# Hedgehog attention and Mish layers on one core: reordering the norm, the key folds and a statistic in the first block

## The chip, the core and the metric

The program runs on one core of a Trainium2 chip. The trace names its engines PE (TensorE, matmul), PEld (its weight loads), DVE (VectorE), ACT (ScalarE), POOL (GpSimd) and SP (SyncE, which issues all transfers here). Each engine works through its own queue in the order in which the compiled program holds it, and stops at an instruction whose wait is not yet fulfilled; nothing behind that instruction on the same engine goes ahead of it. The metric is the device time of one launch in microseconds (us), the median of several.

## The reference

The input `x` has 2048 rows of 640 numbers. Twice over, two layers are applied to it, each of them added to its own input:

```python
x = x + A(layernorm(x))      # linear attention with the Hedgehog feature map
x = x + B(layernorm(x))      # dense 640 -> 1536, Mish, dense 1536 -> 640
```

In A, `q`, `k` and `v` are 32 heads of 20 columns each, from one product with `wqkv`. For queries and keys, each head's 20 numbers are multiplied by the head's own 20x20 matrix `w_phi`, and the features are the softmax of the result beside the softmax of its negative. Then `kv = phi_k^T v` and `z = sum(phi_k)` over all rows, the output is `phi_q kv / (phi_q z)`, and `wo` follows.

## The kernel before

All rows are worked in 8 blocks of 256 rows (`NB`), a block being two tiles (`BT`) of 128 rows. Each fp32 operand of a product is split in a high part and the rest (`hi`, `lo`, tiles ending in h and l), and a product is three matmuls in a narrower form: high by high, high by low, low by high. So 128 rows by 640 columns of depth into one half of the columns takes 5 x 3 = 15 matmuls (`project_half`, L385); a `project` (L376) does both halves. Their rows in the trace are L391.

`w_phi` does not act on the features. It is folded into the query and key weights once, at the start: for each of the 5 row blocks `k` of the weights, and for each half `c` of their columns, `fold_part` (L257) issues three matmuls of a block of `wqk_t` with the block diagonal of `w_phi` (L262 in the trace; each is recorded as two). I call this fold (k,c). `fold_end` (L272) then evicts the fold's bank: ACT copies it to the high weights (L275), and DVE subtracts that copy from the bank to get the low weights (L276). The query weights are `r2h`, `r2l`, the key weights `r1h`, `r1l`; the right 640 columns of the `r1` tiles are the value weights.

PSUM is used in two kinds of tiles: two `mm` tiles of two banks each, and four `one` tiles of one bank. The framework that records the program puts in the waits: an instruction that writes an `mm` tile waits for what was recorded earlier and reads or writes that tile, the other bank included.

The order of work at the start of layer 0 (`attend_first`, L435):

- Written out by hand (`with written()`, L500 to 557): load x of block 0, the statistics of its rows on DVE (`norm_stats`) with their scaling on POOL (`norm_scale`), fold the first halves of the query weights, normalise the two tiles of rows (`xn`: one on ACT at L529, one on DVE at L530), turn them on PE (`Transposed.step`, L325, with the copies L330/L331), the first half of the first query product `q0`, fold the second halves of the query weights beside the splitting of the value weights (`make_v`, L142/L143), and the second half of `q0`.
- From L565 on, the loop over blocks. Its order within a queue is made by a planner that simulates the block of code with costs of its own (`schedule_with_timeline_sim`); `issue_after` gives it an order that it has to keep. Block 0 takes `q0, v0, v1, k0, q1, k1`. `fold_phi(kv_ws, ...)` folds the key weights between `v1` and `k0`: 10 folds, (0,0) (1,0) (2,0) (3,0) (0,1) (1,1) (2,1) (3,1) (4,0) (4,1), even `k` in the two banks of an `mm` tile and odd `k` in two `one` tiles.
- Beside these, for each coming block its x is loaded, its statistics are taken (`fetch_normed`, L438: four `BATCH_NORM_STATS2` of L295 on DVE, two aggregates of L297, three small steps on POOL, two scalings of L307 on DVE), its rows are normalised on ACT (L134) and turned on PE.
- `features` (L402) makes phi of one tile of rows: an ACT copy out of PSUM, two reductions (L416), two subtractions (L417, L419), an exponential on ACT, a sum (L425), a reciprocal (L426) and a product on POOL (L427).

The second layer and all later stages (attend_second, dense) have the same order before and after the change.

Of the kernel before, what the change touches and what calls it, by code (L numbers as in the profile page):

```python
# [1 line left out]

# [6 lines left out]
F32 = mybir.dt.float32  # L9
F32R = mybir.dt.float32r  # L10
AF = mybir.ActivationFunctionType
ALU = mybir.AluOpType
# [32 lines left out]
def kernel(  # L45
# [22 lines left out]
    def mm_tile():  # L68
        return psum.tile([P, 2, 512], F32, tag="mm", name="mm", bufs=2)

    def one_tile():
        return psum.tile([P, 512], F32, tag="one", name="one", bufs=4)
# [41 lines left out]
    x1_d = dram.tile([S, D], F32, name="x1_d")  # L114
    x2_d = dram.tile([S, D], F32, name="x2_d")

    last_act, in_written, last_low, last_load, last_recip = [None], [False], [None], [None], [None]

    @contextmanager
    def written():  # L120
# [136 lines left out]
    def fold_part(ps, k, t, bd, raw):  # L257

        r, rows = raw[t]
        heads = rows // DH  # L260
        n = DL * (6 * (t % 3) if t < 5 else 10)
        nc.tensor.matmul(ps[:, n:n + heads * DL].rearrange("p (j d) -> p j d", d=DL), r[:rows, k * P:(k + 1) * P],  # L262
                         bd[:rows, t, :rows].rearrange("p (j d) -> p j d", d=DH)[:, :, :DL], start=True, stop=True)

    def shift_phi(bd, ts):

# [5 lines left out]
    def fold_end(ws, ps, k, c):  # L272
        n0, n1 = (0, 18 * DL) if c == 0 else (18 * DL, QK)
        hi, lo = ws[k][0][:, n0:n1], ws[k][1][:, n0:n1]
        nc.scalar.activation(hi, ps[:, :n1 - n0], AF.Copy)  # L275
        nc.vector.tensor_tensor(lo, ps[:, :n1 - n0], hi.bitcast(F32), op=ALU.subtract)  # L276

    def fold_phi(ws, bd, raw):

        pss = {}  # L280
        for k, c in ((0, 0), (1, 0), (2, 0), (3, 0), (0, 1), (1, 1), (2, 1), (3, 1), (4, 0), (4, 1)):
            if c == 0:
                mm = None if k % 2 else mm_tile()
                pss[k] = [one_tile(), one_tile()] if k % 2 else [mm[:, 0], mm[:, 1]]
            ps = pss[k][c]
            for t in range(3 * c, 3 * c + 3):
                fold_part(ps, k, t, bd, raw)
            fold_end(ws, ps, k, c)


# [9 lines left out]
    def norm_scale(b, mvs):  # L300

        ve = work.tile([P, BT], F32, tag="ve", name="ve", bufs=2)
        for t in range(BT):
            nc.gpsimd.tensor_scalar(ve[:, t:t + 1], mvs[t][:, 1:2], LN_EPS, 1.0, op0=ALU.add, op1=ALU.mult)
        nc.gpsimd.tensor_tensor(stats[:, b, 0], ve, neg_half, op=ALU.pow)
        for t in range(BT):
            nc.vector.scalar_tensor_tensor(stats[:, b, 1, t:t + 1], mvs[t][:, 0:1], -1.0,  # L307
                                           stats[:, b, 0, t:t + 1], op0=ALU.mult, op1=ALU.mult)
# [76 lines left out]
    def project_half(ps, xts, t, ws, col, c, ks=range(KD), w=HC):  # L385
        sl = slice(t * P, (t + 1) * P)
        cs = slice(col + c * w, col + (c + 1) * w)
        for k in ks:
            h, l, wh, wl = xts.hs[k], xts.ls[k], ws[k][0][:, cs], ws[k][1][:, cs]
            for n, (a, r) in enumerate(((h, wh), (h, wl), (l, wh))):  # L390
                nc.tensor.matmul(ps[:, :w], a[:, sl], r, start=(k == 0 and n == 0),  # L391
                                 stop=(k == KD - 1 and n == 2))

    def both(ps, w=HC):

# [39 lines left out]
    def attend_first(layer, x_src, first):  # L435


        def fetch_normed(b):  # L438
            if layer:
                return load_turned(n2_d[b], [row_tile] * 3, nc.gpsimd)  # L440
            xt = fetch(x_src, b) if b > 1 else early
            norm_scale(b, [norm_stats(t, xt) for t in range(BT)])
            return xt

        pending = []
# [53 lines left out]
        if first is None:  # L499
            with written():  # L500
                xt = fetch(x_src, 0)
                bd = big_tile()[:120, :720].rearrange("p (t c) -> p t c", t=6)
                nc.sync.dma_start(bd[:, :3], phi_bd[:, :3])
                raw_q = load_raw(0, range(3))

                nc.vector.memset(bd[:80, 5, :80], 0.0)
                nc.sync.dma_start(bd[:40, 5, :40], phi_bd[80:120, 4, 80:120])
                nc.sync.dma_start(bd[40:80, 5, 40:80], phi_bd[:40, 5, :40])
                nc.sync.dma_start(bd[:, 3:5], phi_bd[:, 3:5])
                shift_phi(bd, slice(0, 3))  # L510
                raw_q += load_raw(0, range(3, 6))
                kv_ws = [r1_pair(k) for k in range(KD)]
                raw_v = [fetch_v(k) for k in range(KD)]
                raw = load_raw(1)
                early = fetch(x_src, 1)
                mvs = [norm_stats(t, xt) for t in range(BT)]
                norm_scale(0, mvs)
                shift_phi(bd, slice(3, 5))
                shift_phi(bd, 5)

                q_ws = [r2_pair(k) for k in range(KD)]
                mm = [mm_tile(), mm_tile()]
                pcs = [mm[0][:, 0], mm[0][:, 1], mm[1][:, 0], mm[1][:, 1], one_tile()]
                for t in range(3):
                    for k in range(KD - 1):
                        fold_part(pcs[k], k, t, bd, raw_q)
                fold_end(q_ws, pcs[0], 0, 0)
                xn = [row_tile() for _ in range(BT)]
                act(xn[0], xt[:, 0, :], AF.Identity, bias=stats[:, 0, 1, 0:1], scale=stats[:, 0, 0, 0:1])  # L529
                nc.vector.tensor_scalar(xn[1], xt[:, 1, :], stats[:, 0, 0, 1:2], stats[:, 0, 1, 1:2],  # L530
                                        op0=ALU.mult, op1=ALU.add)
                fold_end(q_ws, pcs[1], 1, 0)
                fold_end(q_ws, pcs[2], 2, 0)
                nxt = Transposed(xn)
                nxt.step()
                fold_end(q_ws, pcs[3], 3, 0)
                nxt.step()
                for t in range(3):
                    fold_part(pcs[4], 4, t, bd, raw_q)
                nxt.step()  # L540
                fold_end(q_ws, pcs[4], 4, 0)
                mm = mm_tile()
                q0 = [mm[:, 0], mm[:, 1], mm]
                project_half(q0[0], nxt, 0, q_ws, 0, 0, w=QC)

                def make_v(k):
                    split(kv_ws[k][0][:, D:2 * D], kv_ws[k][1][:, D:2 * D], raw_v[k])

                for k in range(KD):
                    ps = one_tile()  # L550
                    for t in range(3, 6):
                        fold_part(ps, k, t, bd, raw_q)
                    fold_end(q_ws, ps, k, 1)
                    if k > 0:
                        make_v(k - 1)
                project_half(q0[1], nxt, 0, q_ws, 0, 1, w=QC)
                make_v(KD - 1)
            nc.sync.dma_start(mask, bass.AP(tensor=head_mask.tensor, offset=head_mask.offset,
                                            ap=[[1, 120], [120 * (DH + 1), 3]]))
        else:  # L560
            nxt, kv_ws, turn = first
            with tc.issue_after(last_load[0]):
                load_k_weights(kv_ws)
            q_ws = load_q_weights()
        for b in range(NB):  # L565
# [15 lines left out]
            for n, (kind, t) in enumerate(order):  # L581
                t = int(t)
                i = b * BT + t
                if b == 0 and n == (1 if layer else 3):
                    if layer == 0:
                        fold_phi(kv_ws, bd, raw)
                    kva = one_tile()
                    nc.vector.memset(kva[:, :360], 0.0)
                if b == NB - 1 and n == 3:
                    loaded = {0: load(0)}  # L590
                if b + 1 < NB:
                    if n == 0:
                        xt = fetch_normed(b + 1)
                    elif n == 2:
                        nxt = xt if layer else normed(b + 1, xt)
                    elif n > 2:
                        nxt.step()
                g = {"k": lambda: keys(xts, i, vs[t]), "q": lambda: queries(xts, i, q0 if i == 0 and not layer else None),
                     "v": lambda: values(xts, i, vs[t])}[kind]()
                if b == NB - 1 and n == 3:  # L600
                    advance()
                    next(g)
                else:
                    next(g)
                    if layer and b == 0 and n == 0:
                        turn()
                    advance()
                pending.append(g)
# [414 lines left out]
```

## Time and profile before

| what | value |
|---|---|
| median of 3 runs | 1363.8 us (1362.54 to 1365.35) |
| the profiled execution | 1361.69 us, its span 1359.7 us |
| PE busy | 1349.6 us, 99% of the span |
| DVE busy | 1057.4 us, 78% |
| ACT busy | 576.0 us, 42% |
| POOL busy | 464.0 us, 34% |
| transfers | 174.11 MB, mean 128 GB/s |

The profile has several views: the page with the busy time of each engine and the span cut in slices, the list of waits (who stood still, and what ended it), and the timeline (the instructions of an engine in order of time: start, duration, engine, line, operation, output <- input, shape, count of merged instructions, and in brackets the idle time ahead of it with what ended it). A duration in the timeline overlaps the next instruction's start a little, so the distance between two starts is the better price of a step in a full queue. Most of the change lies in the first 50 us of 1360.

### The profile page before, as it was taken

To read this page: it belongs to the slowest core of one execution; us is meant where nothing else is said; L and a number is where in the kernel's file an instruction comes from. 1 tells how busy PE (TensorE), PEld (TensorE's weight loads), DVE (VectorE), ACT (ScalarE), POOL (GpSimd) and SP (SyncE) were. 2 spreads that over 40 slices of the span, in tenths; PEclk is the share of its full clock that TensorE was granted. 3 is DMA by queue.
4 is the path that set the end of the run, shared out by engine and by line. 5 is a ranking of instruction groups with operands and counts; after the bars stand their busy time and mean duration, and the time that the engine had idled before them with its cause. 6 is when DMAs were issued, how large, how long until landed. Compare 5 with 4: busy or idle time off the path is not lost.

```text
span 1359.7 us, 30969 instructions
## 1 busy us (share of the span) xinstructions
PE 1349.6 (99%) x12896; PEld 1338.2 (98%) x12896; DVE 1057.4 (78%) x1799; ACT 576.0 (42%) x967; POOL 464.0 (34%) x417
## 2 busy tenths in 40 slices
PE   9999999999999999999999999999999999999998
PEld 9999999999999999999999999999999999999998
DVE  5888988876687887778769788779668776676775
ACT  4444344322454545445443334332236444444443
POOL 2355644444222222222225555634351211111111
PEclk9999999999999999999999999999999999999999
DMA  9543443797714442244563534559964221233200
GB/s 338 156 103 79 98 96 81 206 287 274 222 40 98 117 117 69 61 106 100 145 209 81 119 79 91 96 120 289 289 246 125 78 72 39 86 98 97 73 26 20
DMA packets 352629, 174.11 MB, mean 128 GB/s; under 512 B 287449, under 2 KB 324041, under 8 KB 352489
## 3 DMA queue, kind: packets, MB, share of 16 engines
q1 hardware_dynamic: 352489, 172.14, 46.7%
q8 instruction: 101, 1.65, 0.5%
q14 instruction: 39, 0.32, 0.1%
HBM read 106.23 MB, written 65.86 MB: 127 GB/s over the span
## 4 chain that ended last, share of the span: by engine, by line
PE 94%; DVE 3%; POOL 1%; ACT 0%; issue 0%; DVEq 0%; POOLq 0%
PE mm L391 25%; PE mm L851 25%; PE one L809 25%; PE one L391 12%; PE mm L686 3%; PE one L325 2%; PE one L464 2%; DVE r L425 1%; DVE m L416 0%; DVE r L419 0%; POOL big L427 0%; DVE big L417 0%; DVE r1l L276 0%; POOL xtl L331 0%; POOL r L427 0%
## 5 line engine op out<-in xcount | busy, mean ns | idle before, releaser
L851 PE MATMUL mm<-r2h,ol 128*128 128x320 f32 x1280 | 304.8, 309 | 0.0
L835 POOL TENSOR_TENSOR ol<-big,ol 128x512 fp32r<-128x512 f32 (+1 forms) x98 | 131.1, 1338 | 477.2 <-ACT ol L834 419.1
L809 PE MATMUL one<-xtl,r1h 128*128 128x256 f32 x960 | 268.2, 279 | 0.0
L809 PE MATMUL one<-xth,r1l 128*128 128x256 f32 x960 | 268.0, 279 | 0.0
L809 PE MATMUL one<-xth,r1h 128*128 128x256 f32 x960 | 265.9, 279 | 0.0
L851 PEld LDWEIGHTS mm<-r2h,ol 128*128 128x128 f32 x1280 | 219.2, 188 | 0.0
L851 PE MATMUL mm<-r2l,ol 128*128 128x320 f32 x640 | 197.3, 309 | 0.0
L391 PE MATMUL mm<-r1h,xth 128*128 128x304 f32 (+1 forms) x600 | 185.1, 309 | 1.5 <-DVE r1l L276 1.5
L391 PE MATMUL mm<-r1l,xth 128*128 128x304 f32 (+1 forms) x600 | 183.8, 306 | 0.0
L391 PE MATMUL mm<-r1h,xtl 128*128 128x304 f32 (+1 forms) x600 | 183.5, 306 | 0.2 <-POOL xtl L331 0.2
L809 PEld LDWEIGHTS one<-xtl,r1h 128*128 128x128 f32 x960 | 180.4, 188 | 0.0
L809 PEld LDWEIGHTS one<-xth,r1l 128*128 128x128 f32 x960 | 180.4, 188 | 0.0
L809 PEld LDWEIGHTS one<-xth,r1h 128*128 128x128 f32 x960 | 179.6, 188 | 0.0
L824 DVE TENSOR_SCALAR big<-big 128x512 f32<-128x512 f32 (+1 forms) x98 | 56.6, 578 | 110.0 <-ACT big L822 109.8
L851 PEld LDWEIGHTS mm<-r2l,ol 128*128 128x128 f32 x640 | 120.2, 188 | 0.0
L834 ACT ACTIVATE ol<-big 128x512 fp32r<-128x512 f32 (+1 forms) x98 | 60.9, 622 | 137.8 <-DVE big L833 137.8
L826 ACT ACTIVATE big<-big,two 128x512 f32<-128x512 f32 (+1 forms) x98 | 70.1, 716 | 116.0 <-DVE big L825 115.9
L822 ACT ACTIVATE big<-one,b1s 128x256 f32<-128x256 f32 x192 | 80.9, 468 | 88.5 <-PE one L809 88.0
L427 POOL TENSOR_TENSOR r<-r,r 128x1280 f32<-128x1280 f32 x32 | 77.2, 2413 | 119.1 <-DVE r L426 101.6
L391 PEld LDWEIGHTS mm<-r1h,xth 128*128 128x128 f32 x600 | 112.8, 188 | 2.6 <-DVE r1l L276 1.7
L391 PEld LDWEIGHTS mm<-r1h,xtl 128*128 128x128 f32 x600 | 112.8, 188 | 0.4 <-POOL xtl L331 0.4
L391 PEld LDWEIGHTS mm<-r1l,xth 128*128 128x128 f32 x600 | 112.8, 188 | 0.1
(142 smaller groups left out, 3118.0 us busy)
## 6 DMA issues: line engine op xcount, KB each, us to landing
e_d<-r SPq DMA_DIRECT2D x128, 160.0 KB, 4.0
big<-e_d SPq DMA_DIRECT2D x32, 640.0 KB, 7.6
x_d<-xt SPq DMA_DIRECT2D x23, 640.0 KB, 3.8
xt<-x_d SPq DMA_DIRECT2D x22, 640.0 KB, 5.5
n_d<-xn SPq DMA_DIRECT2D x168, 80.0 KB, 2.3
xt<-in_x SPq DMA_DIRECT2D x16, 640.0 KB, 4.4
xn<-x_d SPq DMA_DIRECT2D x28, 320.0 KB, 4.4
v<-n_d SPq DMA_DIRECT2D x30, 256.0 KB, 3.1
```

The lines of the kernel that those rows point to most:

```text
L325: nc.tensor.transpose(ps[:, c, t * P:(t + 1) * P], self.rows[t][:, (c0 + c) * P:(c0 + c + 1) * P], ident)
L391: nc.tensor.matmul(ps[:, :w], a[:, sl], r, start=(k == 0 and n == 0), stop=(k == KD - 1 and n == 2))
L427: nc.gpsimd.tensor_tensor(eg, eg, r.unsqueeze(2).to_broadcast([P, 2 * H, DH]), op=ALU.mult)
L464: nc.tensor.matmul(kva[32 * j:32 * j + DH + 1, 40 * r:40 * r + 40], v[:, (DH + 1) * h:(DH + 1) * (h + 1)], e[:, 40 * h:40 * h + 40], start ...
L686: nc.tensor.matmul(po[64 * q:64 * q + 64, c, GW * j:GW * j + w], phs[g][:n, s0:s0 + 64], kvb[:n, g, :w], start=True, stop=True)
L809: nc.tensor.matmul(ph[:, j, :], l, r, start=(n == 0), stop=(n == 3 * KD - 1))
L822: exps[0] = nc.scalar.activation(part(ta, 0)[:, j - js.start], ph[:, j, :], AF.Exp, bias=b1s[:, 2 * pr + j:2 * pr + j + 1]).ins
L824: nc.vector.tensor_scalar_min(e, e, E_CAP)
L826: nc.scalar.activation(r, n, AF.Ln, bias=two)
L834: nc.scalar.activation(ah[:, js], n, AF.Copy)
L835: nc.gpsimd.tensor_tensor(al[:, js], n, ah[:, js].bitcast(F32), op=ALU.subtract)
L851: nc.tensor.matmul(pys[t][:, c, :HC], l[:, j, sl], r, start=(f == 0 and n == 0), stop=(f == KF - 1 and n == 2))
```

## The change

It has four parts, all in layer 0, block 0:

1. The two normalisations `xn` of block 0 stand ahead of the eviction of query fold (0,0) instead of behind it.
2. The key folds go in two groups. The folds (0,0) (1,0) (2,0) (3,0) go ahead of `v1`, the other six, (4,0) (0,1) (1,1) (2,1) (3,1) (4,1), behind it. In each group the first four go into the four banks of the two `mm` tiles, in that order; the last two of the second group go into `one` tiles.
3. `issue_after` now holds each fold and each product of block 0 behind the product recorded before it (`last_product`), and, for the last two steps of the block, the pending feature work behind the last key eviction (`last_fold`).
4. The statistics of block 3 are held behind the last key eviction.

```diff
-    def fold_phi(ws, bd, raw):
-        pss = {}
-        for k, c in ((0, 0), (1, 0), (2, 0), (3, 0), (0, 1), (1, 1), (2, 1), (3, 1), (4, 0), (4, 1)):
-            if c == 0:
-                mm = None if k % 2 else mm_tile()
-                pss[k] = [one_tile(), one_tile()] if k % 2 else [mm[:, 0], mm[:, 1]]
-            ps = pss[k][c]
-            for t in range(3 * c, 3 * c + 3):
-                fold_part(ps, k, t, bd, raw)
+    def fold_phi(ws, bd, raw, parts):
+        mm = [mm_tile(), mm_tile()]
+        banks = [mm[0][:, 0], mm[0][:, 1], mm[1][:, 0], mm[1][:, 1]]
+        for n, (k, c) in enumerate(parts):
+            ps = banks[n] if n < 4 else one_tile()
+            with tc.issue_after(last_product[0]):
+                for t in range(3 * c, 3 * c + 3):
+                    fold_part(ps, k, t, bd, raw)
             fold_end(ws, ps, k, c)
...
-            norm_scale(b, [norm_stats(t, xt) for t in range(BT)])
+            with (tc.issue_after(last_fold[0]) if b == 3 else nullcontext()):
+                norm_scale(b, [norm_stats(t, xt) for t in range(BT)])
...
-                fold_end(q_ws, pcs[0], 0, 0)
                 xn = [row_tile() for _ in range(BT)]
                 act(xn[0], xt[:, 0, :], AF.Identity, bias=stats[:, 0, 1, 0:1], scale=stats[:, 0, 0, 0:1])
                 nc.vector.tensor_scalar(xn[1], xt[:, 1, :], stats[:, 0, 0, 1:2], stats[:, 0, 1, 1:2],
                                         op0=ALU.mult, op1=ALU.add)
+                fold_end(q_ws, pcs[0], 0, 0)
...
+                if b == 0 and layer == 0 and n in (2, 3):
+                    fold_phi(kv_ws, bd, raw, ((0, 0), (1, 0), (2, 0), (3, 0)) if n == 2 else
+                             ((4, 0), (0, 1), (1, 1), (2, 1), (3, 1), (4, 1)))
                 if b == 0 and n == (1 if layer else 3):
-                    if layer == 0:
-                        fold_phi(kv_ws, bd, raw)
                     kva = one_tile()
...
-                if b == NB - 1 and n == 3:
+                if b == 0 and not layer:
+                    with tc.issue_after(last_product[0]):
+                        next(g)
+                    with (tc.issue_after(last_fold[0]) if n > 3 else nullcontext()):
+                        advance()
+                elif b == NB - 1 and n == 3:
```

The compiled programs hold the same instructions on each engine. Their orders differ in the first 50 us alone. This is how the queues of the changed program stand in the part that matters (line numbers of the kernel before; "evict" is a fold's ACT copy or DVE subtraction):

```
PE   query folds (0,1)..(4,1) | q0 second half, 15 | v0, 30 | fold (0,0) | fold (1,0) | fold (2,0) | fold (3,0)
     | v1, 30 | folds (4,0) (0,1) (1,1) (2,1) (3,1) (4,1) | 4 transposes | k0, 30 | 4 transposes | q1, 30 | 2 transposes | k1
DVE  ...splitting of the value weights | 4 stats of block 1 | 2 reductions L416 of q0 | 2 aggregates
     | 4 stats of block 2 | L419 of q0 | aggregate | evict (0,0) | 2 scalings L307 | aggregate | 2 scalings L307
     | evict (1,0) (2,0) (3,0) | L425 of q0 | evict (4,0) | L426 of q0 | evict (0,1) (1,1) | memset
     | evict (2,1) (3,1) (4,1) | transpose of q0 | 4 stats of block 3 | L331 | ...
ACT  copy of q0 | ones column | 2 copies of v0 | evict (0,0) | 2 normalisations of block 1 | ones column
     | evict (1,0) (2,0) (3,0) | 2 copies of v1 | exponential of q0 | evict (4,0) (0,1) (1,1) (2,1) (3,1) (4,1) | ...
```

And these waits stand in the changed program on PE: fold (1,0) waits for the DVE eviction of fold (0,0), fold (3,0) for that of (2,0), fold (0,1) for that of (4,0), fold (2,1) for that of (1,1). In the kernel before, fold (2,1) waits for the DVE eviction of (2,0) in the same way. On SP the writes of the folded key weights (`wp_d`, L222) go in another order, and all ten stand ahead of the four writes of q0's features (`e_d`, L481); before, the two writes of the last row block and one load of `wo` (L156) stood behind those four.

More of the change, by code (lines that the diff above doesn't have):

```diff
@@ L1 @@
-from contextlib import ExitStack, contextmanager
+from contextlib import ExitStack, contextmanager, nullcontext
 import concourse.bass as bass
@@ L115 @@
     x2_d = dram.tile([S, D], F32, name="x2_d")
-    last_act, in_written, last_low, last_load, last_recip = [None], [False], [None], [None], [None]
+    last_act, in_written, last_low, last_load, last_recip, last_fold, last_product = (
+        [None], [False], [None], [None], [None], [None], [None])
     @contextmanager
@@ L261, in fold_part @@
         n = DL * (6 * (t % 3) if t < 5 else 10)
-        nc.tensor.matmul(ps[:, n:n + heads * DL].rearrange("p (j d) -> p j d", d=DL), r[:rows, k * P:(k + 1) * P],
+        ins = nc.tensor.matmul(ps[:, n:n + heads * DL].rearrange("p (j d) -> p j d", d=DL), r[:rows, k * P:(k + 1) * P],
                          bd[:rows, t, :rows].rearrange("p (j d) -> p j d", d=DH)[:, :, :DL], start=True, stop=True)
+        last_product[0] = ins.ins
     def shift_phi(bd, ts):
@@ L275, in fold_end @@
         nc.scalar.activation(hi, ps[:, :n1 - n0], AF.Copy)
-        nc.vector.tensor_tensor(lo, ps[:, :n1 - n0], hi.bitcast(F32), op=ALU.subtract)
-    def fold_phi(ws, bd, raw):
-        pss = {}
-        for k, c in ((0, 0), (1, 0), (2, 0), (3, 0), (0, 1), (1, 1), (2, 1), (3, 1), (4, 0), (4, 1)):
-            if c == 0:
-                mm = None if k % 2 else mm_tile()
-                pss[k] = [one_tile(), one_tile()] if k % 2 else [mm[:, 0], mm[:, 1]]
-            ps = pss[k][c]
-            for t in range(3 * c, 3 * c + 3):
-                fold_part(ps, k, t, bd, raw)
+        last_fold[0] = nc.vector.tensor_tensor(lo, ps[:, :n1 - n0], hi.bitcast(F32), op=ALU.subtract).ins
+    def fold_phi(ws, bd, raw, parts):
[6 more added lines that the diff above has]
+                    fold_part(ps, k, t, bd, raw)
             fold_end(ws, ps, k, c)
@@ L390, in project_half @@
             for n, (a, r) in enumerate(((h, wh), (h, wl), (l, wh))):
-                nc.tensor.matmul(ps[:, :w], a[:, sl], r, start=(k == 0 and n == 0),
-                                 stop=(k == KD - 1 and n == 2))
+                last_product[0] = nc.tensor.matmul(ps[:, :w], a[:, sl], r, start=(k == 0 and n == 0),
+                                                   stop=(k == KD - 1 and n == 2)).ins
     def both(ps, w=HC):
```

## The prediction

> **What bounds the kernel now.** I read the page first, then PE's list of waits, then the timeline of each engine over the first 60 us.
>
> ```profile
> span 1359.7 us, 30969 instructions
> PE 1349.6 (99%) x12896; PEld 1338.2 (98%) x12896; DVE 1057.4 (78%) x1799; ACT 576.0 (42%) x967; POOL 464.0 (34%) x417
> PEclk9999999999999999999999999999999999999999
> ...
> PE mm L391 <- DVE r1l L276: 1.5, 1, 1.5
> PE mm L262 <- DVE r1l L276: 1.1, 1, 1.1
> PE one L325 <- ACT xn L131: 0.9, 1, 0.9
> PE mm L686 <- issue: 0.4, 1, 0.4
> ```
>
> PE is the bound, at full clock in all slices. Once it has started it stands still for 1.5 + 1.1 + 0.9 us in block 0, all in what the change touches, and for under 1 us in the other 1300 us. This says two things. The change can gain at most some 3.5 us (0.26%). And whatever idle time it gives PE comes out at the end in full, because no later slack takes it up. So the question is what PE waits for in the new order.
>
> ```profile
> 15.24 0.56 PE L262 MATMUL one<-big,raw 120*128 120x114 f32 x4
> ...
> 24.43 0.31 PE L391 MATMUL one<-r1l,xth 128*128 128x320 f32 x1
> 30.00 0.31 PE L391 MATMUL one<-r1h,xtl 128*128 128x320 f32 x1
> 30.15 0.82 PE L262 MATMUL one<-big,raw 120*128 120x114 f32 x6
> 30.80 0.83 PE L262 MATMUL mm<-big,raw 120*128 120x114 f32 x6
> ...
> 35.34 0.67 PE L262 MATMUL mm<-big,raw 120*128 120x114 f32 x4 [1.05 <-DVE r1l L276]
> 39.47 0.41 PE L391 MATMUL mm<-r1h,xth 128*128 128x304 f32 x1 [1.49 <-DVE r1l L276]
> 44.44 0.30 PE L391 MATMUL mm<-r2h,xth 128*128 128x304 f32 x1
> ```
>
> Prices from here: a value matmul 0.147 us (38 steps between 24.43 and 30.00), so a `v` of 30 is 4.4; a fold 0.65 (30.15 to 30.80); `k0` 4.2 (39.47 to 44.44 is 4.97 for its 30 matmuls with fold (4,1) of 0.65 among them, and 0.1 goes to the restart). The row of 35.34 is fold (2,1) waiting for the DVE eviction of (2,0), which lies in the other bank of its `mm` tile. That wait, 1.05 us, is the one that the new order meets four times. The row of 39.47 is `k0` waiting for an eviction that stood behind block 3's statistics:
>
> ```profile
> 20.68 0.43 DVE L276 TENSOR_TENSOR r2l<-one,r2h 128x266 fp32r<-128x266 f32 x1
> 24.16 1.67 DVE L295 BATCH_NORM_STATS2 bn<-xt 128x6 f32<-128x320 f32 x4 [1.15 <-DMA xt<-in_x]
> 25.75 0.33 DVE L297 BATCH_NORM_AGGREGATE mv<-bn 128x2 f32<-128x12 f32 x2
> 25.99 0.87 DVE L295 BATCH_NORM_STATS2 bn<-xt 128x6 f32<-128x320 f32 x2
> 26.78 1.53 DVE L416 TENSOR_REDUCE m<-r 128x32 f32<-128x640 f32 x2
> 28.23 0.88 DVE L295 BATCH_NORM_STATS2 bn<-xt 128x6 f32<-128x320 f32 x2
> 29.22 0.82 DVE L419 TENSOR_TENSOR r<-m,r 128x640 f32<-128x640 f32 x1
> 29.95 0.20 DVE L297 BATCH_NORM_AGGREGATE mv<-bn 128x2 f32<-128x12 f32 x1
> 31.24 0.23 DVE L307 SCALAR_TENSOR_TENSOR stats<-mv,stats 128x1 f32<-128x1 f32 x2 [1.09 <-POOL stats L305]
> 32.96 1.49 DVE L425 TENSOR_REDUCE r<-r 128x64 f32<-128x1280 f32 x1 [1.48 <-ACT r L134]
> 34.36 0.50 DVE L276 TENSOR_TENSOR r1l<-one,r1h 128x342 fp32r<-128x342 f32 x1
> 37.48 1.61 DVE L295 BATCH_NORM_STATS2 bn<-xt 128x6 f32<-128x320 f32 x4
> 39.00 0.42 DVE L276 TENSOR_TENSOR r1l<-mm,r1h 128x266 fp32r<-128x266 f32 x1
> ```
>
> DVE is full from 24.16 on, when x of block 1 lands, and works in queue order. Starts give the prices: four statistics 1.59, two aggregates 0.24, two reductions 1.45, L419 0.73.
>
> **The change part by part.** All times are on the clock of the profiled execution before.
>
> *Norm ahead of the eviction.*
>
> ```profile
> 9.55 0.46 ACT L275 ACTIVATE r2h<-mm 128x342 fp32r<-128x342 f32 x1 [7.55 <-PE mm L262]
> 10.04 0.51 DVE L276 TENSOR_TENSOR r2l<-mm,r2h 128x342 fp32r<-128x342 f32 x1 [1.68 <-ACT r2h L275]
> 10.71 0.79 ACT L275 ACTIVATE r2h<-mm 128x342 fp32r<-128x342 f32 x2
> 10.87 1.25 PE L325 MATMUL one<-ident,xn 128*128 128x128 f32 x8 [0.91 <-ACT xn L131]
> 11.71 0.60 ACT L131 ACTIVATE xth<-one 128x512 fp32r<-128x512 f32 x1 [0.21 <-PE one L325]
> ```
>
> ACT stood idle 7.55 us ahead of 9.55, so the normalisation goes into idle time and the transposes lose their wait of 0.91. What is late next is the copy of the first turned tile (11.71): it stays behind the evictions of (0,0), (1,0) and (2,0). (1,0) shares its tile with (0,0) and waits for the DVE eviction, which ends at 10.55; then 0.79 for the two: the copy starts at about 11.3. Gain 0.4, of 0 to 0.9.
>
> *Second half of q0.* Its 14th matmul needs the low weights of query fold (4,1), evicted at 20.68 + 0.43 = 21.11, now about 20.7. PE comes there earlier: five folds from 14.85 on (15.24 - 0.4) are 3.3, 13 matmuls at 0.14 are 1.8, so at 19.95. Before, value matmuls filled that gap; `issue_after` now holds them behind. Cost 0.8. `v0` runs from 21.0 to 25.4, fold (0,0) to 26.1.
>
> *Wait A, fold (1,0).* It waits for the DVE eviction of (0,0), which the planner put behind the statistics of two blocks: 24.16 + 1.59 (four of block 1) + 1.45 (L416) + 0.24 + 1.59 (four of block 2) + 0.73 (L419) + 0.12 (aggregate) + 0.50 (eviction) = 30.4. PE stands from 26.1 to 30.4: 4.3 us. Queued behind are three folds and all of `v1`, none of which needs that eviction but (1,0).
>
> *Wait B, fold (3,0).*
>
> ```profile
> 29.27 1.74 ACT L134 ACTIVATE xn<-xt,stats 128x640 f32<-128x640 f32 x2 [2.27 <-DVE stats L307]
> 31.03 0.74 ACT L134 ACTIVATE v<-one 128x320 f32<-128x320 f32 x2
> 31.66 1.26 ACT L134 ACTIVATE r<-r 128x1280 f32<-128x1280 f32 x1
> 32.82 0.45 ACT L275 ACTIVATE r1h<-one 128x342 fp32r<-128x342 f32 x1
> ```
>
> Folds (1,0) and (2,0) take PE to 31.7. The eviction of (2,0) on ACT stands behind that of (1,0) and the two normalisations of block 1. These wait for the scalings behind eviction (0,0), so they start at about 30.45; normalisations and ones column 1.76 (29.27 to 31.03), two evictions 0.8, then 0.50 on DVE: 33.6. PE loses 1.9. (POOL's way to block 2's scalings, 1.29 from 29.95 to 31.24, ends at 31.8 and is hidden under ACT.)
>
> *Wait C, fold (0,1).* Fold (3,0) and `v1` run to 38.7, (4,0) to 39.35. The DVE eviction of (4,0) stands behind L425 of q0, that behind q0's exponential on ACT, and that behind the copies of `v1`, the second of which can start at about 38.9: 0.3 + 1.26 + 1.40 (32.96 to 34.36) + 0.50 = 42.4. PE loses 3.1.
>
> *Wait D, fold (2,1).* Folds (0,1) and (1,1) end at 43.75; (2,1) waits for ACT and DVE to evict (1,1), 0.45 + 0.43 and some 0.2 until ACT sees the matmul: 44.85. PE loses 1.1.
>
> *To the same point.* Folds (2,1), (3,1), (4,1): 46.8. Four transposes 0.5 (10.87: eight in 1.25, the last ending late), `k0` 4.2: 51.5. The six transposes that stood ahead of 44.44 before come later now, 0.7: 52.2 against 44.44, **7.8 us later**. By waits it is 4.3 + 1.9 + 3.1 + 1.1 + 0.8, less 1.05 + 1.49 taken away and 0.4 at the head, 8.3; idle time counts from modelled ends of matmuls, so I take the 7.8.
>
> *Block 3's statistics later:*
>
> ```profile
> 50.02 0.16 POOL L407 MEMSET r<- 128x32 f32 x1 [7.56 <-DMA e_d<-r]
> 91.48 1.72 ACT L134 ACTIVATE xn<-xt,stats 128x640 f32<-128x640 f32 x2
> ```
>
> This takes 1.6 of DVE from ahead of an eviction, which is in the sum. They are used first at 91.48, so behind 48 they cost nothing. *SP and POOL:* q0's writes now start some 10 us later (transpose of q0 at 48), behind all key weight writes; the POOL memset that waits for them stood 7.56 us idle at 50.02 and moves to about 59, against 8 us for everything else: 1 to 2 us of that feature's slack, no PE.
>
> The profiled execution would go to 1361.7 + 7.8 = 1369.5. The median of the runs stands 2.1 above that execution, so I predict 1371.6.
>
> **The rivals.**
>
> *Waits by bank (not slower).* If a fold into the other bank did not wait, A to D would fall: (1,0) to (3,0) and `v1` run to 32.4, six folds and four transposes to 37, when (4,0) is also evicted; 37 + 4.2 + 0.7 = 41.9, 2.5 ahead of before: 1361.3. [...] Against it stand the 1.05 us at 35.34 and the waits that the compiled program holds. It tips to not slower once A to D cost under 2.6 together. 4%.
>
> *A cold PE.* No row before shows PE idle over 1.5 us, so none prices 4.3. From nothing, to half speed from wait A to the end of `v1`: the two folds are hidden by B, fold (3,0) and `v1` would take 5.05 more, 1376.7. I take nothing, since the clock row is at 9 beside the waits of 1 to 1.5. [...] 14%.
>
> *Another landing of x of block 1.* A follows it one to one. Earlier helps until DVE is free, 2.0 before 24.16 (its 1.15 idle, the eviction moved away, the head): 1369.6. Later costs as much. 10%.
>
> *How the numbers follow.* The sum as it stands 72%, 1370 to 1373.2 with 1 us for its parts and the runs' own scatter; cold PE 14%; the landing 10%; by bank 4%. The range 1368.5 to 1375.5 leaves out the last and the worst of the cold case. A change of 0.2% (2.7 us) is about what can be told here: slower 0.94, within 0.04, faster 0.02.
>
> **What would show it.** The list of PE's waits should name DVE r1l L276 for about 10 us in four waits of 4.3, 1.9, 3.1 and 1.1, and DVE r2l L276 for 0.8; the transposes' 0.9 and the 1.5 ahead of `k0` should be gone; q1's first matmul should start at about 52. I am wrong if fold (1,0) starts before 29, if PE's clock drops below 9 in the first two slices, or if PE shows new waits behind 60 us.

## The result and the profile after

| | before | after |
|---|---|---|
| median | 1363.7 us (1362.54 to 1365.35, 4 runs) | 1377.7 us (1377.06 to 1379.35, 4 runs) |
| ratio | | 1.0105, 95% interval 1.0091 to 1.0119 |
| the profiled execution, its span | 1361.69, 1359.7 | 1377.06, 1375.2 |
| start of q1's first matmul | 44.44 | 58.48 |

The change costs 14.0 us where 7.8 were forecast. Nearly all of it is in block 0: q1's first matmul starts 14.04 us later. Behind that point the profiled execution takes 1316.7 us (1375.2 less 58.48), where that of the kernel before takes 1315.3, and its largest new wait there is 0.63 us, at 933.73. The page of the kernel after, with its slices and its waits:

```profile
span 1375.2 us, 30965 instructions
...
PEclk9799999999999999999999999999999999999999
...
PE mm L263 <- DVE r1l L278: 8.8, 4, 3.2
...
PE mm L263 <- DMA raw<-in_wqk_t: 0.5, 1, 0.5
PE mm L392 <- DVE r2l L278: 0.4, 1, 0.4
```

The four waits are there, 8.8 us in all, and so is that of q0's second half. New beside them is the 7 in the second slice of the clock row. The stretches of 5 us show where (after the name of the stretch: busy time and count on PE, PEld, DVE, ACT and POOL, the granted clock, the DMA share, GB/s):

```profile
30.00:35.00 5.00, 3.33 (x20) 3.15 (x21) 1.33 (x5) 2.65 (x6) 0.88 (x2) 0.68 0.89 324
35.00:40.00 5.00, 5.00 (x25) 5.00 (x24) 0.51 (x1) 0.73 (x2) 0.00 (x0) 0.64 0.01 4
40.00:45.00 5.00, 2.03 (x16) 1.85 (x16) 2.33 (x3) 1.94 (x3) 0.00 (x0) 1.00 0.02 3
45.00:50.00 5.00, 4.05 (x22) 3.84 (x22) 1.55 (x5) 1.18 (x3) 2.36 (x1) 0.55 0.64 238
50.00:55.00 5.00, 5.00 (x24) 5.00 (x23) 3.31 (x7) 1.38 (x3) 0.22 (x2) 0.50 0.92 307
55.00:60.00 5.00, 5.00 (x36) 5.00 (x36) 2.65 (x9) 1.17 (x2) 1.08 (x3) 0.93 1.08 292
```

From 35 to 40 and from 50 to 55 PE has no idle time at all, and yet it finishes only 24 or 25 matmuls where the stretch from 55 to 60, which has none either, holds 36: for most or all of the time it runs at half clock. The clock records of the trace put it at 0.5 from 31.82 to 38.65 and from 45.47 to 55.71. The profile shows one run, but the mean granted clock is 0.992 or 0.993 in all four, where the runs of the kernel before have 0.997 to 1.000. PE's timeline of the kernel after, the four waits and the first matmuls of `v1`, `k0` and `q1`:

```profile
29.92 1.59 PE L263 MATMUL mm<-big,raw 120*128 120x114 f32 x12 [3.19 <-DVE r1l L278]
33.18 1.63 PE L263 MATMUL mm<-big,raw 120*128 120x114 f32 x6 [1.67 <-DVE r1l L278]
34.48 0.61 PE L392 MATMUL one<-r1h,xth 128*128 128x320 f32 x1
...
35.42 0.47 PE L392 MATMUL one<-r1h,xth 128*128 128x320 f32 x1
35.69 0.47 PE L392 MATMUL one<-r1l,xth 128*128 128x320 f32 x1
...
40.85 0.82 PE L263 MATMUL mm<-big,raw 120*128 120x114 f32 x6
44.63 0.67 PE L263 MATMUL mm<-big,raw 120*128 120x114 f32 x4 [2.97 <-DVE r1l L278]
47.69 1.14 PE L263 MATMUL mm<-big,raw 120*128 120x114 f32 x4 [0.95 <-DVE r1l L278]
48.62 0.63 PE L263 MATMUL mm<-big,r 80*128 80x76 f32 x2
49.05 1.06 PE L263 MATMUL one<-big,raw 120*128 120x114 f32 x4
...
52.32 0.60 PE L392 MATMUL mm<-r1h,xth 128*128 128x304 f32 x1
...
58.48 0.39 PE L392 MATMUL mm<-r2h,xth 128*128 128x304 f32 x1
```

In order: A 3.19, B 1.67, C 2.97, D 0.95. Behind B a value matmul takes 0.27 (35.42 to 35.69) where the kernel before has 0.147; fold (3,0) takes 1.30 (33.18 to 34.48) and fold (2,1) 1.36 (47.69 to 49.05) where 0.65 is usual.

DVE's timeline of the kernel after shows why A is shorter than forecast: x of block 1 landed at 23.70 and not at 24.16, and the eviction of (0,0) came as much sooner.

```profile
23.70 1.67 DVE L296 BATCH_NORM_STATS2 bn<-xt 128x6 f32<-128x320 f32 x4 [1.18 <-DMA xt<-in_x]
...
29.40 0.46 DVE L278 TENSOR_TENSOR r1l<-mm,r1h 128x342 fp32r<-128x342 f32 x1
```

From landing to fold (1,0) it is 6.22 us, against 6.24 in the forecast (30.4 less 24.16).

### The profile page after: what moved, and what is told of

Its sections match the earlier page's. It is cut to its first block, busy times and chain, and to the rows that moved or that the text cites. A ratio compares the mean times of both kernels' runs of the same rounds, so it can differ in the third digit from the quotient of the medians.

```text
span 1375.2 us, 30965 instructions
## 1 busy us (share of the span) xinstructions
PE 1357.6 (99%) x12896; PEld 1344.4 (98%) x12896; DVE 1060.5 (77%) x1799; ACT 577.1 (42%) x967; POOL 462.8 (34%) x417
## 4 chain that ended last, share of the span: by engine, by line
PE 90%; DVE 4%; DMA 3%; POOL 2%; ACT 1%; issue 1%; SPq 0%; DVEq 0%; POOLq 0%
PE mm L859 25%; PE one L817 24%; PE mm L392 24%; PE one L392 11%; PE mm L694 2%; PE one L326 2%; PE one L466 1%; DMA raw<-in_w 1%; DVE r L426 1%; DMA xt<-in_x 1%; DVE m L417 1%; POOL r1l L165 1%; DMA raw<-in_wqk_t 0%; DVE r L420 0%; DMA big<-e_d 0%
```

## The experiments

The theory: the waits cost what the forecast says, some 7 us, and the other half is the half clock that the idle time brings on. The rivals: the waits alone cost the 14 us; the order of the folds does, whatever they wait for; the other two parts of the change share in it.

### Filling the waits

```diff
+        fill = {(1, 0): 25, (3, 0): 13, (0, 1): 24, (2, 1): 7}
...
         for n, (k, c) in enumerate(parts):
             ps = banks[n] if n < 4 else one_tile()
+            for _ in range(fill.get((k, c), 0)):
...
+                with tc.issue_after(last_product[0]):
+                    last_product[0] = nc.tensor.transpose(warm_ps[0][:, :P], ident, ident).ins
```

> The changed kernel with dummy transposes of the identity on PE ahead of folds (1,0), (3,0), (0,1) and (2,1): 25, 13, 24 and 7 of them, into a PSUM tile that nothing reads. The folds wait for the same evictions as before, but PE isn't idle meanwhile. Theory (half of the 14.0 us is the half clock that follows the idle time): the clock stays at 1.0 through block 0, q1's first matmul starts about 7 us earlier than in the changed kernel, at 51 to 52.5, and the kernel takes 1370 to 1372. Rival (the waits alone cost the 14 us, and the half clock is only in the records): 1377 to 1378, q1 at 58.

Measured: 1372.8 us (1370.63 to 1374.25), ratio 1.0063 [1.0047, 1.0078]. From this kernel, DVE's row of the landing of x of block 1, PE's timeline and the stretches:

```profile
24.51 1.67 DVE L303 BATCH_NORM_STATS2 bn<-xt 128x6 f32<-128x320 f32 x4 [1.73 <-DMA xt<-in_x]
...
26.82 2.89 PE L292 MATMUL one<-ident 128*128 128x128 f32 x25
30.73 1.59 PE L263 MATMUL mm<-big,raw 120*128 120x114 f32 x12 [1.01 <-DVE r1l L278]
...
39.17 0.82 PE L263 MATMUL mm<-big,raw 120*128 120x114 f32 x6
...
52.53 0.39 PE L399 MATMUL mm<-r2h,xth 128*128 128x304 f32 x1
```
```profile
35.00:40.00 5.00, 5.00 (x38) 5.00 (x37) 0.52 (x1) 1.48 (x4) 0.00 (x0) 1.00 0.14 56
...
50.00:55.00 5.00, 5.00 (x39) 5.00 (x38) 4.26 (x11) 1.17 (x2) 1.08 (x3) 1.00 1.01 364
```

The folds still wait for their evictions, as the transposes add no product; but the clock stays at 1.00, and q1 starts at 52.53 in place of 58.48. In this execution x of block 1 landed at 24.51, 0.81 later than in the kernel after. Counted from that landing, q1 starts after 28.02 us here and after 34.78 there (58.48 less 23.70). So the waits and the order are worth 7.3 of the 14.0, and the half clock 6.76. Of these, 2.49 have come by the start of fold (4,0) (40.85 less 23.70 is 17.15; here 39.17 less 24.51 is 14.66), the other 4.27 behind C.

The total came out 0.8 above what the theory gave: of the 5.95 us by which q1 starts sooner, 4.96 are left at the end. New waits of 0.4 to 1.2 us stand at 265 to 268 and at 927 to 992 in its profiled execution. Other runs below likewise keep less of what they save in block 0. Why such waits come wasn't followed up, so the split into 7.3 and 6.76 holds for q1's start and not to the microsecond for the total.

### Filling the first two alone

```diff
-        fill = {(1, 0): 25, (3, 0): 13, (0, 1): 24, (2, 1): 7}
+        fill = {(1, 0): 25, (3, 0): 13}
```

> The run with the dummy transposes again, with those ahead of folds (1,0) and (3,0) alone, 25 and 13 of them; PE stands idle ahead of (0,1) and (2,1) as in the changed kernel. Theory (each half-clock stretch follows its own idle time, and the first is worth 2.5 and the second 4.3 us or less): full clock up to the third wait, half clock for 2 or 3 stretches of 3.41 us behind it, q1's first matmul at 55.5 to 57, 3 to 4.5 us behind the run with all four filled and 1.5 to 3 ahead of the changed kernel. Rival (one cause for both, the first wait starts it): full clock throughout, q1 at 52.5.

Measured: 1376.6 us (1375.35 to 1377.72), ratio 1.0101 [1.0084, 1.0118]; q1 starts at 54.86, with the landing at 24.02. The stretches of this kernel, cut where its clock records change:

```profile
40.73:44.14 3.41, 1.56 (x12) 1.41 (x12) 2.46 (x4) 0.56 (x3) 1.13 (x1) 1.00 0.00 0
44.14:47.56 3.42, 2.59 (x12) 2.59 (x13) 1.33 (x4) 0.70 (x2) 1.22 (x1) 0.50 0.86 319
47.56:50.97 3.41, 3.41 (x17) 3.41 (x17) 1.85 (x3) 1.38 (x3) 0.23 (x2) 0.50 1.04 335
```

Full clock up to C, half behind it: each stretch has its own idle time as cause, and the rival falls. From the landing to q1 it is 30.84, so this second stretch costs 2.82, less than the 4.27 in the kernel after: it lasts two steps of 3.41 here and three there. My bounds for q1 were 0.6 too high for that reason. The total moved by 1.2 only, and q1 by 3.62: in the profiled execution this kernel meets another stop, of 2.08 us ahead of 271.93, and 3.41 us of half clock behind it.

### Folds of their own tiles

```diff
+    fold_mm = []
...
-        mm = [mm_tile(), mm_tile()]
-        banks = [mm[0][:, 0], mm[0][:, 1], mm[1][:, 0], mm[1][:, 1]]
+        if not fold_mm:
+            fold_mm.extend([mm_tile(), mm_tile()])
+        side = 0 if parts[0] == (0, 0) else 1
         for n, (k, c) in enumerate(parts):
-            ps = banks[n] if n < 4 else one_tile()
+            ps = fold_mm[n][:, side] if n < 2 else one_tile()
...
-                             ((4, 0), (0, 1), (1, 1), (2, 1), (3, 1), (4, 1)))
+                             ((0, 1), (1, 1), (2, 1), (3, 1), (4, 0), (4, 1)))
```

> The changed kernel with the first four folds in tiles of their own: (0,0) in one mm tile, (1,0) in the other, (2,0) and (3,0) in one tiles; the second group puts (0,1) and (1,1) into the other halves of the two mm tiles and the rest into one tiles. Waits A and B have nothing to wait for any more. Theory (the shared tile makes A and B): folds (0,0) to (3,0) run without a wait, 2.6 us, PE keeps full clock through v1; what is left is a wait ahead of (2,1) or of k0 of at most 3 us, and the kernel takes 1362 to 1368, by how much of that is left and whether the clock holds. Rival (the order of the folds against v1 costs the time, whatever the tiles): over 1373.

Measured: 1361.4 us (1360.23 to 1363.10), ratio 0.9984 [0.9975, 0.9993]: 1.8 us faster than the kernel before, better than I expected. PE's timeline in this kernel, whose list of waits names no key fold any more:

```profile
25.35 1.49 PE L263 MATMUL mm<-big,raw 120*128 120x114 f32 x12
26.68 1.50 PE L263 MATMUL one<-big,raw 120*128 120x114 f32 x12
...
32.43 0.57 PE L263 MATMUL mm<-big,raw 120*128 120x114 f32 x4
...
41.54 0.30 PE L395 MATMUL mm<-r2h,xth 128*128 128x304 f32 x1
```

All four first halves run without a stop ahead of `v1`, the second group runs without a stop behind it, and q1 starts 2.9 us sooner than in the kernel before. The evictions come no sooner (that of (0,0) ends at 29.87, as in the kernel after at 29.86); nothing on PE needs them yet. So the folding by halves is no loss as such: what cost time was that two folds which follow each other closely shared a tile (A 3.19 and B 1.67 in the kernel after, no wait here). For A and B that is shown, as in the first group nothing but the tiles changed. For C and D it is argued, since the run also moves (4,0) behind the other folds of the second group, and no run keeps that order with other tiles.

### The other parts and the folds, each alone

The kernel before, with the norm ahead and the statistics later:

```diff
...
-            norm_scale(b, [norm_stats(t, xt) for t in range(BT)])
+            with (tc.issue_after(last_fold[0]) if b == 3 else nullcontext()):
+                norm_scale(b, [norm_stats(t, xt) for t in range(BT)])
...
-                fold_end(q_ws, pcs[0], 0, 0)
                 xn = [row_tile() for _ in range(BT)]
...
+                fold_end(q_ws, pcs[0], 0, 0)
```

> The kernel before with two parts of the change alone: the normalisation of block 0 ahead of the first eviction, and block 3's statistics behind the last eviction of a key weight. The folds stay as they were. Theory (these two parts are good or neutral, the folds' order costs all of it): the wait of 1.49 us ahead of k0 is gone or under 0.5, the one of 0.9 ahead of the first transposes too, and the kernel takes 1361.5 to 1363, 0.7 to 2 us under the kernel before. Rival (one of these two parts is itself part of the loss): 1365 or more, with a new wait on PE in the first 60 us.

Measured: 1362.3 us (1359.77 to 1365.80), ratio 0.9992 [0.9982, 1.0002], which can't be told from no change. In the profile both waits are gone, 0.83 stays ahead of (2,1), and q1 starts at 42.58, 1.86 sooner. In the profiled execution all of it is spent again, by a stop of 1.69 us for a load at 916.56 and 3.41 us of half clock behind it, which the profile of the kernel before doesn't have:

```profile
913.75:917.16 3.41, 1.72 (x43) 1.41 (x44) 1.51 (x6) 0.42 (x1) 0.00 (x0) 1.00 1.01 346
917.16:920.57 3.41, 3.41 (x36) 3.00 (x32) 2.59 (x7) 1.47 (x3) 0.00 (x0) 0.50 1.04 355
```

The changed kernel without these two parts:

```diff
-            with (tc.issue_after(last_fold[0]) if b == 3 else nullcontext()):
-                norm_scale(b, [norm_stats(t, xt) for t in range(BT)])
+            norm_scale(b, [norm_stats(t, xt) for t in range(BT)])
...
+                fold_end(q_ws, pcs[0], 0, 0)
                 xn = [row_tile() for _ in range(BT)]
...
-                fold_end(q_ws, pcs[0], 0, 0)
```

> The changed kernel without its first and its last part: the first eviction is ahead of the normalisation again, and block 3's statistics are where the planner puts them; only the folding by halves is left. Theory (the folds' order makes the four waits and the half clock that follows): the four waits are there, the third up to 1.6 us longer with the statistics ahead of it, the clock drops to 0.5 twice, and the kernel takes 1377 to 1381. Rival (the other two parts share in the loss): under 1375.

Measured: 1376.7 us (1375.95 to 1377.06), ratio 1.0102 [1.0087, 1.0117]. The four waits are 2.64, 1.49, 2.97 and 0.95, the clock is at 0.5 from 31.05 for 6.83 us and from 44.71 for 10.24, and q1 starts at 58.06. The folds cost all of the loss, within the scatter of the runs. C did not grow with the statistics ahead of it, as I had thought possible.

### DVE's queue

The changed kernel with its tiles and its order, but with the statistics of blocks 1 and 2 behind the eviction of (2,0):

```diff
+    first_low = [None]
...
             fold_end(ws, ps, k, c)
+            if (k, c) == (2, 0):
+                first_low[0] = last_fold[0]
+                with tc.issue_after(last_fold[0]):
+                    norm_scale(1, [norm_stats(t, early) for t in range(BT)])
...
+            if b == 1:
+                return xt
-            with (tc.issue_after(last_fold[0]) if b == 3 else nullcontext()):
+            with tc.issue_after(first_low[0]) if b == 2 else (tc.issue_after(last_fold[0]) if b == 3 else nullcontext()):
                 norm_scale(b, [norm_stats(t, xt) for t in range(BT)])
...
```

> The changed kernel, tiles and order of the folds as they are, with the statistics of blocks 1 and 2 held back on DVE until the eviction of (2,0) has been issued, so that the evictions of (0,0), (1,0) and (2,0) stand ahead of them there. Theory (waits A and B are the queue of DVE ahead of the evictions that the shared tiles make PE wait for): A and B shrink to about 1.0 each, C and D stay at about 3 and 1; that is 3 us less of waits, q1 at 55.5 or, where the first drop of the clock goes too, at 52 to 53; the kernel takes 1370 to 1375. Rival (A and B are set by something else, the landing of x or ACT): A over 2.5 us, and 1376 or more.

Measured: 1374.1 us (1372.42 to 1374.49), ratio 1.0081 [1.0066, 1.0096]. PE's timeline of this kernel:

```profile
27.10 1.59 PE L264 MATMUL mm<-big,raw 120*128 120x114 f32 x12 [1.09 <-DVE r1l L279]
29.79 0.92 PE L264 MATMUL mm<-big,raw 120*128 120x114 f32 x6 [1.09 <-DVE r1l L279]
39.37 1.13 PE L264 MATMUL mm<-big,raw 120*128 120x114 f32 x4 [3.58 <-DVE r1l L279]
43.16 1.14 PE L264 MATMUL mm<-big,raw 120*128 120x114 f32 x4 [0.95 <-DVE r1l L279]
...
53.11 0.39 PE L397 MATMUL mm<-r2h,xth 128*128 128x304 f32 x1
```

A and B are 1.09 each, the bare way through ACT and DVE (1.05 in the kernel before). The 2.1 us that A had above it, and the 0.6 of B, were DVE's queue ahead of the evictions. With them the first half-clock stretch goes; the one behind C stays, from 39.08 for 10.24 us. C itself is 0.6 longer than in the kernel after: the two normalisations of block 1, held back as well, start at 33.72 on ACT, ahead of the copies of `v1` and the exponential that C waits for. Of the 5.4 us by which q1 starts sooner, 3.6 are left at the end; the profiled execution has stops of 0.8 to 1.0 us at 329 and 928 to 929, and 3.41 us of half clock behind the last.

### Stops of known length

The kernel before, with stops in the dense part of the first layer (layer 0 in the code), where PE otherwise has no idle time (from 460 to 700 in the kernel before it is busy for all 240 us). First eleven stops of different lengths (left out here: the matmuls of the dense part are held behind the stop recorded before them):

```diff
...
+                if i in stops:
+                    ps = one_tile()
+                    with tc.issue_after(last_mm[0]):
+                        mark[0] = nc.tensor.transpose(ps[:, :P], fill, ident).ins
+                    for _ in range(stops[i]):
+                        with tc.issue_after(mark[0]):
+                            nc.gpsimd.memset(fill, 0.0)
+                    with tc.issue_after(mark[0]):
+                        mark[0] = nc.tensor.transpose(ps[:, P:2 * P], fill, ident).ins
```

> The kernel before with eleven stops of PE in the first layer's dense part, where PE has no other idle time: at each, PE transposes a tile of zeros, POOL then clears that tile n times, and PE transposes it again and only then goes on; n is 1, 4, 8, 12, 16, 20, 2, 6, 10, 14 and 18, some 28 us apart, so PE should stand for 0.5 to 6 us. Theory 1 (idle time of about 3 us is enough for the half clock, though no window of 3.4 us is empty): stops up to 1.5 us leave the clock at 1.0, those over 3 us are followed by 3.4 to 10 us at 0.5, and each of these costs 1.7 to 5 us beside its own length. Theory 2 (only a window of 3.4 us that is wholly idle does it): half clock only behind stops of 3.4 us and longer, for certain from 6.8. Theory 3 (the half clock of block 0 comes from its mix of folds and from the start, not from the waits): the clock stays at 1.0 behind all of them.

Measured: 1423.3 us, one run. The stops were 0.32, 0.58, 1.78, 2.15, 2.35, 2.68, 4.31, 5.78, 6.00, 6.40 and 6.48 us. The clock stayed at 1.0 behind 0.32, 0.58, 1.78 and 2.68, and fell to 0.5 behind the others, 2.15 and 2.35 among them: for 3.41 us behind the 2.15, 2.35 and 4.31, for 6.83 behind the four longest, where the first half-clock step still held 1.0 to 2.1 us of the stop. Theories 2 and 3 fall. Theory 1 fits the stops that it speaks of, but says nothing on those between 1.5 and 3 us. The length alone doesn't decide either, or 2.68 would have done it. The stretches of half clock begin and end on one grid of 3.413 us: three of them begin at 441.20, 475.34 and 509.47, each ten steps behind the one before. Cut on that grid, around the stop of 2.15 (ends at 441.28) and that of 2.68 (ends at 643.76):

```profile
437.79:441.20 3.41, 1.33 (x10) 1.06 (x8) 3.38 (x7) 1.29 (x2) 1.61 (x8) 1.00 0.00 0
441.20:444.62 3.42, 3.34 (x16) 3.35 (x17) 0.83 (x2) 0.63 (x1) 1.30 (x2) 0.50 0.00 0
639.18:642.59 3.41, 1.90 (x14) 1.63 (x12) 3.41 (x7) 1.88 (x4) 1.16 (x6) 1.00 0.00 0
642.59:646.01 3.42, 2.25 (x19) 2.25 (x20) 1.38 (x2) 0.64 (x1) 2.11 (x6) 1.00 0.00 0
```

The shorter stop lies in one window, 61% of it (2.08 of 3.41), and the window behind runs 16 matmuls (28 fit in at full clock, below). The longer one is cut by the grid into 44% and 34%, and the clock stays at 1.00. To see whether the share decides, eleven stops of nearly one length:

```diff
-STOPS = {4: 1, 8: 4, 12: 8, 16: 12, 20: 16, 24: 20, 28: 2, 32: 6, 36: 10, 40: 14, 44: 18}
+STOPS = {4 * j: 4 + j % 4 for j in range(1, 12)}
```

> The kernel before with eleven stops of PE in the dense part of layer 1 again, all of nearly the same length: n is 5, 6, 7, 4, 5, 6, 7, 4, 5, 6 and 7 clearings, 1.8 to 2.7 us. In the run with stops from 0.3 to 6.5 us the clock changed in steps of 3.41 us, and what told a drop from none was the largest part of one such window in which PE stood idle: 61% and 69% dropped it, 48% and 44% didn't. Theory (a window with more than half idle halves the clock of the next): stops of one and the same length drop it or not by where they fall, about 6 of the 11 here, and each follows the share of its window with a border between 48% and 61%. Rival (the length of the stop decides): all over some length drop it and all under it don't.

Measured: 1403.4 us, one run; stops of 1.37 to 3.00 us. Of the pair that tells the two theories apart, the first stop is 1.82 us and ends at 599.59, the second is 2.74 and ends at 662.42:

```profile
596.26:599.67 3.41, 1.58 (x12) 1.31 (x11) 3.41 (x4) 1.43 (x3) 2.02 (x5) 1.00 0.33 52
599.67:603.08 3.41, 3.41 (x17) 3.41 (x18) 3.41 (x9) 0.87 (x2) 0.09 (x1) 0.50 0.87 137
...
657.70:661.11 3.41, 1.98 (x14) 1.71 (x12) 2.97 (x7) 1.76 (x3) 1.25 (x4) 1.00 0.86 229
661.11:664.53 3.42, 2.11 (x18) 2.11 (x19) 2.52 (x3) 0.63 (x1) 1.22 (x5) 1.00 0.79 123
664.53:667.94 3.41, 3.41 (x28) 3.41 (x28) 0.60 (x2) 0.84 (x2) 1.20 (x1) 1.00 0.00 0
```

The shorter, which filled 53% of one window, halved the clock of the next; the longer, 42% of one and 38% of the other, did not. Three of the eleven dropped it, with 67, 56 and 53% of a window; the eight others reached at most 42%. I had expected about six: the grid cut more of them in two. In this run the length of a stop didn't decide; the share of a window did.

## Why the prediction was right or wrong

**Bound and direction: right.** What idles PE in block 0 came out at the end: q1 14.04 later, the median 14.0. That the two agree so well is partly luck: the two profiled executions differ by 15.4, and the run with all four waits filled starts q1 8.1 later than the kernel before and takes 9.6 more, as later waits came on top.

**The four waits: right.** They stand at the named folds with the named releasers, 3.19, 1.67, 2.97 and 0.95 against 4.3, 1.9, 3.1 and 1.1. A lost 0.46 to the landing of x of block 1 and some 0.6 to PE itself, which came to fold (1,0) at 26.73 and not at 26.1. The first moves the end of the wait as well, the second only its start. Where the clock stayed full, q1 started 28.02 us behind that landing; the prediction has 52.2 less 24.16, 28.04. So the sum of all edits was right as far as it was a sum of waits and durations at full clock. That it is right to 0.02 is luck: from the landing to fold (2,1) it gives 20.69 where that run took 20.96 (45.47 less 24.51), and the rest was 0.3 shorter than forecast.

**Head: 0.4 was about right, and hidden.** With the norm ahead alone (in the run with the two parts) the copy of the first turned tile starts at 11.40 against 11.71, 0.3 sooner. In the kernel after it starts at 11.56, since the query weights landed later there (0.5 of wait at 8.0). **q0's second half:** 0.39 of wait in place of 0.8; PE came later and the eviction did too.

**Block 3's statistics, SP and POOL: right.** The 1.49 ahead of `k0` is gone, and the longest wait of PE behind 60 us in the kernel after is 0.63. The POOL memset that waits for q0's writes starts at 62.69, 12.67 later than before, and PE 14.04: no slack was lost.

**The step that failed: "I take nothing, since the clock row is at 9 beside the waits of 1 to 1.5."** The cold PE stood among the rivals with 14%, for A alone, at nothing to 5.05. It came, and twice: 2.5 behind A and B, 4.3 behind C and D, 6.8 in all. The sign that the prediction named for it, a clock below 9 in the first two slices, is there. Four things were wrong in the step.

- *The row did not carry the conclusion.* Waits of 1.05 and 1.49 us fill at most 44% of a window of 3.41. They show that 44% was harmless there, and say nothing on 3 us. In the runs with known stops one of 1.82 us dropped the clock (53% of a window), one of 2.74 did not (42 and 38%), and all five of 4.31 us and longer did.
- *The row can't show what was asked of it.* A slice is 34 us, and a 9 stands for 90% or more, so a slice can hold 6.8 us of half clock and still show a 9. In the first run with known stops the row has a 9 in all 40 slices, with seven stretches of half clock.
- *It was priced for A alone.* C, forecast at 3.1, filled 75% of a window (42.06 to 45.47) and was the dearer one. A was cut by the grid, 49% before 28.41 and 44% behind; with the start of B, 0.31 us more, the second window came to 53%, and the clock was at 0.50 from its end.
- *The price was in the trace.* I wrote that no row prices a cold PE. The timeline of PE in the kernel before has its first matmuls, behind the 1.34 us of idle time with which the profile begins:

```profile
1.34 5.95 PE L92 MATMUL one<-ident 128*128 128x128 f32 x30 [1.34 <-POOL ident masks.py:199]
```

That is 0.2 us for a transpose; the same 128x128 transposes of the identity take 0.116 in the run with the filled waits (25 in 2.89). Step by step these 30 take 0.213 us up to 6.41, where the first clock record at 1.0 begins, and 0.110 behind it. The factor of two stood there.

**Rivals.** Waits by bank: refuted by the four waits in the kernel after, and by the run with other tiles, in which they are gone. The sum that the rival gave, q1 at 41.9 and 1361.3 us, is close to what that run measured (41.54 and 1361.4), since none of its key folds has to wait for a tile. The cold PE: it was the right rival. Its half speed stood without a row (in the kernel after a value matmul takes 0.27 behind B, for 0.147 before), and its worst case, 1376.7, lies near the measured 1377.7, but by luck, as it puts 5.05 us behind A where 2.5 came, and nothing behind C, where 4.3 came. The landing: it came 0.46 sooner, and moved the end of A by as much.

## What to carry to other kernels

Price a new wait on PE in two steps: its own length, and the half clock that can stand behind it. Here the half clock took 2.5 us behind the waits of 3.19 and 1.67 and 4.3 behind those of 2.97 and 0.95, while the clock stayed at 1.0 with the waits of 1.05 and 1.49 in the kernel before. Before a product is moved up in the order, look whether the tile that it writes still has an eviction ahead of it, and where that eviction stands in its engine's queue; giving the four early folds a place without such a wait, and reordering the later six, turned a loss of 14 us into a gain of 1.8. Where a wait can't be avoided, products that nobody reads are worth a run: here the clock stayed at 1.00 with them, and they won back 6 us in block 0, and 5 at the end.

## What the hardware showed that was not expected

- In the two runs with known stops the clock fell by the share of idle time in one window of the grid, not by the length of a stop: in the dense part 53, 56, 61, 67 and 69% dropped it and up to 48% did not. With folds or small matmuls in the rest of the window the share alone didn't tell: 46% dropped it at 951.25 in the second run with known stops and 49% at 913.75 in the run with the two parts, both with some 40 short matmuls in the window; 49% did not at 24.99 in the kernel after, before the window that did.
- A window with little or no idle time didn't always bring the clock back. Behind a half-clock window in the dense part with 3.07 of its 3.41 us busy the clock was back at 1.0 (475.34, behind the stop of 4.31), and behind one with 1.00 us idle it was not. In the kernel after it was not back behind a full one either:

```profile
45.47:48.89 3.42, 2.47 (x13) 2.26 (x12) 1.23 (x3) 0.78 (x2) 2.07 (x1) 0.50 0.61 226
48.89:52.30 3.41, 3.41 (x18) 3.41 (x18) 0.90 (x3) 1.18 (x3) 0.22 (x2) 0.50 0.89 330
52.30:55.71 3.41, 3.41 (x15) 3.41 (x14) 3.41 (x7) 0.60 (x1) 0.00 (x0) 0.50 1.01 327
```

  The window from 48.89 holds folds and four transposes, without a gap in the records, and the next one was still at 0.50 (the run with the folds alone has the same from 48.12 to 51.53); behind that of `k0`'s split matmuls it was at 1.0, from 55.71. Why it didn't come back at 52.30 stays open. It isn't the transposes as such: in place of idle time they held the clock at 1.00 (25 to 55 us of the run with all four filled), and at the start of the kernel after, where PE does nothing else, their steps go from 0.213 to 0.109 us at 4.51, where the first record at 1.0 begins, behind a window that had 0.24 us idle.
- The grid doesn't start with the program: half clock began at 31.82 in the kernel after and at 31.05 in the one with the folds alone, whose waits stand within 0.5 us of each other. Where a stop fell on the grid decided in the run with stops of nearly one length: 1.82 us dropped the clock and 2.74 did not.
